# Row sums scaled by ScalarE, small VectorE operations as separate steps, longer DMA pieces and a new order in a fused attention and FFN kernel

## The chip, the cores and the metric

The kernel runs on one core of a Trainium2 chip. The time is device microseconds (us) of one execution, the median of several runs. Five engines work side by side and are ordered by semaphores: TensorE (PE, with its weight loads PEld), VectorE (DVE), ScalarE (ACT), GpSimd (POOL) and SyncE (SP), which issues all DMA transfers here.

## The reference, cut to what matters

```python
# q, k, v: 4 batches x 8 heads x 576 positions x 64
q, k = rotate(q), rotate(k)                       # rotary embedding
attn = softmax(q @ k.T / 8)                       # per batch and head
x = concat_heads(attn @ v)                        # 4 x 576 x 512
xn = (x - mean) / sqrt(var + 1e-6) * g_ln
x = x + relu(xn @ w_ch1) @ w_ch2                  # w_ch1 512 x 2048, w_ch2 2048 x 512
gate = sigmoid(causal_conv5(x, conv_w))           # 5 taps per channel
out = (gate * (x @ w_val)) @ w_out                # 512 x 512 each
```

The weights arrive as 64-bit floats, q, k and v as 32-bit floats.

## The kernel before, in words

**Tiles.** Attention goes batch by batch. A batch has 4 pairs of heads, and its 576 queries are cut in four (128, 128, 128, 192, or with the 192 first in odd batches); a pair and a cut is a part, and a part has two or three tiles of 128 queries by all 576 keys, 144 tiles in all. For a tile PE computes scores into PSUM (`a_scores`; plain 32-bit in batch 0, high and low halves in the others), DVE takes the negated row maximum (`a_max`, L537), ACT the exponential (`a_exp`, L543) and a 16-bit high half (`a_hi`, L549), DVE the low half (`a_lo`, L554), SP issues a DMA transpose (`a_turn`, L559), and PE multiplies the transposed pieces with v and a column of ones (`a_pv`, L578 and L581). The tiles of a part form a group with one PSUM buffer `ov`, of which there is one (ring `so=1`). When a group is complete, `a_rd` drains it on DVE: the row sums, in the column of ones, are scaled with the scale of v (L605), inverted (L606), and the outputs multiplied with them (L610); for the lead tile of 64 queries ACT does the last step (`a_lead`, L624). A second form, `a_sum` on ACT in place of L605, is in the code and not in use (`RD_SUM = 9`, over the highest batch number).

**Weights.** W1 and W2 come as 16 blocks of 1 MB of 64-bit floats (`Conv`, L700). Each block is put together into 32-bit floats by two ACT and one DVE pass (`p1`, `p0`, `p2`), then scaled by powers of two and split into 16-bit high and low halves (`conv_hi`, `conv_lo`). The scales come from bounds that PE and DVE work out; `conv_scale` is a chain of small DVE operations. W1 has two scales, one for each four blocks (`E1 = 2`).

**FFN.** 18 blocks of 128 rows: layer norm (`ln_a` to `ln_d`), a DMA transpose, then four times a first matmul group (`f1`, L882, 48 matmuls), ReLU split into halves (`relu`, `hlo`), and a second matmul group (`f2`, L910, 12 matmuls).

**Tail.** Nine blocks of 256 rows. The gate is a scaled copy on ACT (`gate_a`), four taps on DVE in one step (`gate_b`, L1108), each of which adds to the result of the one before, and a sigmoid on ACT (`gate_c`, L1112). Then come the value projection (`val`, L1121), its product with the gate (L1126), its halves, and the output projection (`proj`, L1148).

**Order.** `Plan` is a planner in Python that runs when the kernel is built. Each piece of work is a step with an engine, an estimated time, a rank, the steps it comes after and the buffers it takes from rings. The planner goes through time: on each engine it takes, of the steps that are ready within `NEAR` us, the one of lowest rank. SP may run `AHEAD` us ahead of what it reckons the wire has moved. The ranks are a constant of the kind (`R_...`) plus the number of the tile or block; loads have a lead (`..._LEAD`) subtracted. A step is indivisible: all its instructions stand together on the engine's queue. The instructions are then issued in the planned order, and each engine works through its own in that order.

**Lines that the change touches.** `pow2_below_inverse` (L137), `vmax0` and `vmax` (L447, L459), `a_sum` and `a_rd` (L590, L597), `conv_scale` (L743), `ln_a` (L832), `norm_scale`, `w_scale` and `x_scale` (L978, L994, L1078), `gate_b` (L1105), the loads `load` and `Conv.load` (L309, L698), and the steps that plan them.

Of the kernel before, what the change touches and what calls it, by code (L numbers as in the profile page):

```python
# [39 lines left out]
R_XB, R_XS = 278.66, -364.59  # L40
# [15 lines left out]
class Plan:  # L56
# [91 lines left out]
def pow2_below_inverse_root(nc, pool, bound, factor, name):  # L148

    m = pool.tile([128, 1], F32, name=name + "_m", tag=name + "_m", bufs=1)  # L150
    nc.vector.tensor_scalar(out=m, in0=bound, scalar1=factor, scalar2=1e-30, op0=ALU.mult, op1=ALU.max)
    nc.vector.reciprocal(out=m, in_=m)
    r = pool.tile([128, 1], F32, name=name + "_r", tag=name + "_r", bufs=1)
    nc.vector.tensor_scalar(out=r.bitcast(I32), in0=m.bitcast(I32), scalar1=1, scalar2=0x7F800000, op0=ALU.logical_shift_right, op1=ALU.bitwise_and)
    return r
# [3 lines left out]
def kernel(ctx: ExitStack, tc: tile.TileContext, qk, v, g_ln, w_ch1, w_ch2, w_val, conv_w, w_out, rope, eye, out):  # L159
    nc = tc.nc  # L160
    B, NP = qk.shape[0], qk.shape[1]
    S = qk.shape[5]
# [4 lines left out]
    DFF = w_ch1.shape[1] // 2  # L167
# [14 lines left out]
    TURN = 1050 * RATE  # L182
# [117 lines left out]
    def plan_prep(p):  # L300
# [17 lines left out]
        def load_half(k):  # L318
# [4 lines left out]
            nc.sync.dma_start(out=st["r", 1][:, :, c], in_=qk[b, pr][:, 1, :, c])  # L323
# [164 lines left out]
        if p < NP:  # L488
            v_abs.append(plan.step(ACT, act(640) + 0.09, r, vabs, after=[x0, x1], uses=[vt, vh], row="vabs"))
            v_rest.append((r, vt, vh, vhi, vlo, vturn, bf))  # L490
            if p == NP - 1:
                x = plan.step(PE, 0.3, R_TINY, vsum0, after=v_abs + [c_c], takes=[hp])
                x = plan.step(DVE, 1.0, r - 8, vmax0, after=[x], takes=[sv0], uses=[hp])
# [10 lines left out]
        x = plan.step(DVE, 0.9, r - 8, vmax, after=[x], takes=[sv], uses=[hp])  # L504
# [92 lines left out]
    def a_rd(g):  # L597
# [6 lines left out]
        if b < RD_SUM:  # L604
            nc.vector.tensor_scalar(out=rd[:, 0:w], in0=ov[:, 0:w, D], scalar1=1e-9 * P_SCALE, scalar2=prep_v(p)["sv"], op0=ALU.add, op1=ALU.mult)  # L605
        nc.vector.reciprocal(out=rd[:, 0:w], in_=rd[:, 0:w])  # L606
        if m and b < RD_ACT:
# [55 lines left out]
    for g, ts in enumerate(groups):  # L663
# [12 lines left out]
        x = plan.step(DVE, (0.2 if b >= RD_SUM else 0.44) + (0 if by_act else m * 0.14 + (0.08 if m else 0)), R_OUT + ts[-1], lambda g=g: a_rd(g), after=[last], takes=[] if b >= RD_SUM else [rd], uses=[so, vf["sv"]] + ([rd] if b >= RD_SUM else []))  # L676
# [15 lines left out]
    class Conv:  # L692
# [50 lines left out]
    def conv_scale(w, e):  # L743
        m = wpool.tile([128, 1], F32, name=f"wn{w}{e}")
        nc.vector.tensor_reduce(out=m, in_=wmax.pop((w, e)), axis=AX.X, op=ALU.max)
        r = pow2_below_inverse_root(nc, wpool, m, 1.08 if w else gmax, f"w{w}{e}")
        if w == 0:
            nc.vector.tensor_scalar(out=sg[:, e], in0=g_sb, scalar1=r, scalar2=ROOT * W1_SCALE, op0=ALU.mult, op1=ALU.mult)
            nc.vector.tensor_scalar(out=s1[:, e:e + 1], in0=r, scalar1=ROOT * W1_SCALE, scalar2=None, op0=ALU.mult)
            if e == E1 - 1:  # L750
                nc.vector.tensor_reduce(out=smin[:, 0:1], in_=s1, axis=AX.X, op=ALU.min)
                inverse(srt, s1)
                nc.vector.tensor_scalar(out=srt, in0=srt, scalar1=smin[:, 0:1], scalar2=ROOT * W2_SCALE, op0=ALU.mult, op1=ALU.mult)
                inverse(smin[:, 1:2], smin[:, 0:1])
        else:
            nc.vector.tensor_scalar(out=s2, in0=srt, scalar1=r, scalar2=None, op0=ALU.mult)
            inverse(scl, r)
            nc.vector.tensor_scalar(out=scl, in0=scl, scalar1=1.0 / (ROOT * W2_SCALE * XN_SCALE), scalar2=smin[:, 1:2], op0=ALU.mult, op1=ALU.mult)

# [14 lines left out]
    for w in range(2):  # L774
# [7 lines left out]
        for e in range(ne):  # L782
            convs = []
            for g in range(per * e, per * e + per):
                if w == 0:
                    src = w_ch1[(g % 2) * 256:(g % 2 + 1) * 256, (g // 2) * 1024:(g // 2 + 1) * 1024].rearrange("(a p) n -> p a n", p=128)
                else:
                    src = w_ch2[g * 256:(g + 1) * 256, :].rearrange("(a p) n -> p a n", p=128)
# [19 lines left out]
            x = scale = plan.step(DVE, 1.15 + 0.4 * (w or e == E1 - 1), r, lambda w=w, e=e: conv_scale(w, e), after=[x, c_g, scale], uses=[hp])  # L808
# [23 lines left out]
    def ln_a(n):  # L832
# [145 lines left out]
    def norm_scale(out, squares):  # L978
        nc.vector.tensor_scalar(out=out.bitcast(I32), in0=squares.bitcast(I32), scalar1=-0.5, scalar2=float((127 + 63 + 15) << 23), op0=ALU.mult, op1=ALU.add)
# [278 lines left out]
```

## Time and profile before

| what | value |
|---|---|
| runs | 729.34, 730.87, 731.23 us; median 730.87 |
| the profiled execution's own time | 732.34 us |
| its span, first to last instruction | 730.5 us |
| mean granted TensorE clock | 0.985 |
| busy PE / DVE / ACT | 666.6 / 628.7 / 469.5 us |
| DMA | 103.63 MB in 240089 packets |

A line such as L605 is the line of the kernel before. "Busy" is the time in which an engine had an instruction at work; matmuls overlap, and their ends are modelled, so a busy PE is not PE at its peak. The granted clock is a share of TensorE's full speed. The chain that ended last is followed back from the last instruction, at each step to what released it. DMA issues are those of SP's queue (SPq), and their times run from issue to landing.

### The profile page before, as it was taken

What the parts mean: (1) busy time and instruction counts of PE and PEld (TensorE: products, weight loads), DVE (VectorE), ACT (ScalarE), POOL (GpSimd) and SP (SyncE); (2) the same over time, 40 slices, a digit from 0 to 9 for tenths busy, and PEclk for the clock granted to TensorE, in tenths of its full rate; (3) what the DMA queues carried; (4) which work ended last, traced back from release to release, by engine and by line L of the source; (5) the groups of instructions that cost most, each with busy time, mean ns of one, the idle gap of its engine ahead of it and who ended that gap; (6) DMA issues with size and microseconds to landing.
All of it is one profiled execution on the core that took longest, in us unless ns stands there. A gap on an engine that the chain in (4) does not pass through costs nothing.

```text
span 730.5 us, 19479 instructions
## 1 busy us (share of the span) xinstructions
PE 666.6 (91%) x7953; PEld 497.8 (68%) x7953; DVE 628.7 (86%) x1396; ACT 469.5 (64%) x854; POOL 16.6 (2%) x40
## 2 busy tenths in 40 slices
PE   3565579999999999999999999999999999999997
PEld 1354468855867977778777877778766556677673
DVE  5978989999889999999999978987556999997683
ACT  3967887896765667666667866555289535442352
POOL 0000000000001000000000000000000000000000
PEclk9998889999999999999999999999999999999999
DMA  8999999667678978788888668875661441321021
GB/s 285 244 207 232 265 275 288 130 132 163 122 131 139 167 158 143 170 155 156 163 167 192 126 119 125 152 119 99 128 193 31 58 76 44 91 66 31 1 73 57
DMA packets 240089, 103.63 MB, mean 142 GB/s; under 512 B 211200, under 2 KB 228608, under 8 KB 240000
## 3 DMA queue, kind: packets, MB, share of 16 engines
q1 hardware_dynamic: 240000, 102.39, 68.2%
q8 instruction: 62, 1.02, 0.5%
q14 instruction: 27, 0.22, 0.1%
HBM read 45.73 MB, written 4.72 MB: 69 GB/s over the span
## 4 chain that ended last, share of the span: by engine, by line
PE 56%; DVE 25%; DMA 10%; ACT 5%; issue 3%; SPq 0%; DVEq 0%; ACTq 0%
PE acc L910 18%; PE hp L882 18%; DMA pT<-p 9%; PE sc L532 6%; DVE gt L1108 5%; PE ov L578 5%; PE po L1148 4%; DVE nmx L537 3%; DVE p L554 3%; PE ov L581 2%; PE pv L1121 2%; DVE wall L770 2%; DVE wall L713 1%; DVE gt L1126 1%; DVE raw L335 1%
## 5 line engine op out<-in xcount | busy, mean ns | idle before, releaser
L882 PE MATMUL hp<-xT,wall 128*128 128x128 f16 x3456 | 205.4, 219 | 2.7 <-DVE wall L770 1.3
L882 PEld LDWEIGHTS <-wall 128*128 128x128 f16 x3456 | 195.4, 98 | 10.0 <-issue 4.5
L910 PE MATMUL acc<-wall,hh 128*128 128x512 f16 x544 | 161.9, 379 | 1.5 <-DVE x L914 1.5
L543 ACT ACTIVATE p<-sc,nmx 128x576 f32<-128x576 f32 x144 | 103.8, 738 | 68.5 <-DVE nmx L537 67.8
L554 DVE SCALAR_TENSOR_TENSOR p<-p,p 128x576 f16<-128x576 f32 x144 | 106.3, 752 | 20.7 <-ACT p L549 20.1
L578 PE MATMUL ov<-vh,pT 128*128 128x65 f16 (+1 forms) x1296 | 95.0, 201 | 24.5 <-DMA pT<-p 21.0
L578 PEld LDWEIGHTS <-pT 128*128 128x128 f16 x1296 | 80.6, 101 | 41.8 <-DMA pT<-p 28.4
L537 DVE TENSOR_REDUCE nmx<-sc 128x1 f32<-128x576 f32 x144 | 104.2, 748 | 0.3
L910 PE MATMUL acc<-wall,hl 128*128 128x512 f16 x272 | 103.1, 379 | 0.0
L549 ACT ACTIVATE p<-p 128x576 f16<-128x576 f32 x144 | 95.5, 679 | 7.0 <-DMA pT<-p 5.8
L910 PEld LDWEIGHTS <-hh 128*128 128x128 f16 x544 | 49.4, 98 | 52.1 <-issue 3.2
L1108 DVE SCALAR_TENSOR_TENSOR gt<-xT,cw,gt 128x256 f32<-128x256 f32 (+4 forms) x192 | 71.7, 414 | 3.7 <-ACT gt L1099 1.1
L581 PE MATMUL ov<-vl,pT 128*128 128x64 f16 (+1 forms) x720 | 69.8, 201 | 0.0
L900 DVE SCALAR_TENSOR_TENSOR hl<-hp,hh 128x512 f16<-128x512 f32 x68 | 46.6, 685 | 15.9 <-ACT hh L894 15.5
L894 ACT ACTIVATE hh<-hp 128x512 f16<-128x512 f32 x68 | 40.2, 591 | 31.1 <-PE hp L882 29.4
L581 PEld LDWEIGHTS <-pT 128*128 128x128 f16 x720 | 54.1, 101 | 4.7
L910 PEld LDWEIGHTS <-hl 128*128 128x128 f16 x272 | 26.6, 98 | 32.1
L1148 PE MATMUL po<-woh,gv 128*128 128x512 f16 x144 | 44.3, 379 | 0.0
L1112 ACT ACTIVATE gt<-gt 128x256 f32<-128x256 f32 x36 | 15.0, 416 | 44.2 <-DVE gt L1108 44.1
L1121 PE MATMUL pv<-xh,wvh 128*128 128x256 f16 x144 | 39.2, 273 | 3.8 <-DVE gt L1126 3.8
L335 DVE TENSOR_TENSOR raw<-raw,rope_sb 128x256 f32<-128x256 f32 (+2 forms) x63 | 41.2, 664 | 1.7 <-DMA raw<-in_qk_dram 1.7
L1121 PE MATMUL pv<-xl,wvh 128*128 128x256 f16 x144 | 39.2, 272 | 0.1
(151 smaller groups left out, 939.9 us busy)
## 6 DMA issues: line engine op xcount, KB each, us to landing
raw<-in_qk_dram SPq DMA_DIRECT2D x15, 576.0 KB, 4.6
raw<-in_qk_dram SPq DMA_DIRECT2D x48, 128.0 KB, 2.9
wall<-in_moe_w_ch_dram SPq DMA_DIRECT2D x6, 1024.0 KB, 6.5
xw<-in_moe_w_ch_dram SPq DMA_DIRECT2D x6, 1024.0 KB, 6.9
vt<-in_v_dram SPq DMA_DIRECT2D x16, 320.0 KB, 3.4
out_dram<-x SPq DMA_DIRECT2D x18, 256.0 KB, 2.0
kk<-in_moe_w_ch_dram SPq DMA_DIRECT2D x4, 1024.0 KB, 6.7
raw<-in_qk_dram SPq DMA_DIRECT2D x16, 192.0 KB, 4.1
```

Source lines behind the costliest of these rows:

```text
L335: nc.vector.tensor_tensor(out=a, in0=a, in1=t, op=ALU.mult)
L537: nc.vector.tensor_reduce(out=nmx, in_=sc[:, :, 0:HS], axis=AX.XY, op=ALU.max, negate=True)
L543: nc.scalar.activation(out=p32.rearrange("p (e n) -> p e n", e=2), in_=sc[:, :, 0:HS], func=ACTF.Exp, bias=nmx)
L549: nc.scalar.activation(out=p16[:, 0], in_=p32, func=ACTF.Copy, scale=P_SCALE)
L554: nc.vector.scalar_tensor_tensor(out=p16[:, 1], in0=p32, scalar=P_SCALE, in1=p16[:, 0], op0=ALU.mult, op1=ALU.subtract)
L578: nc.tensor.matmul(o, pT[:, c], vh[:, 2 * c + hs:2 * c + hs + nh], start=(c == 0), stop=(c == 8))
L581: nc.tensor.matmul(o[..., 0:D], pT[:, c], vl[:, 2 * c + hs:2 * c + hs + nh], start=False, stop=False)
L882: nc.tensor.matmul(hp[:, j], w1[:, u, wl * 512 + o:wl * 512 + o + 128], xT[:, xl * KD + c], start=(i == 0), stop=(i == 3 * KD - 1))
L910: nc.tensor.matmul(st["acc"], lw[:, j], w2[:, f + j, lo * 512:lo * 512 + 512], start=(f + j == 0 and i == 0), stop=(f + j == KF - 1 and i ...
L1108: nc.vector.scalar_tensor_tensor(out=gt[:, c0:c1], in0=xT[:, c, HALO + c0 - s:HALO + c1 - s], scalar=col(KT - 1 - s, c), in1=gt[:, c0:c1], ...
L1121: nc.tensor.matmul(pv, lw[:, d, c * 128:(c + 1) * 128], rx[:, d], start=(n == 0), stop=(n == 3 * KD - 1))
L1148: nc.tensor.matmul(po, lw[:, d, sl], rx[:, d, :], start=(n == 0), stop=(n == 3 * KD - 1))
```

## The change

Four things change together.

1. `RD_SUM` is 1 instead of 9: in batches 1 to 3 ACT scales the row sums as they leave PSUM (`a_sum`: one activation with scale and bias), and DVE only inverts them and multiplies. For the bias each preparation of v in those batches has one more 1-element DVE operation.
2. A new kind of step, a chain: the small DVE operations that were one step become one step each, planned with times of their own, so that the planner can lay other work between them. The instructions are those of before. This holds for the divide by the row sums, the scales of v, of W1, W2, w_val and w_out, the layer norm's statistics, the scale of x in the tail and the gate's taps.
3. The 1 MB weight blocks and the queries are laid out in DRAM by the host so that what one transfer brings to a partition is one piece: 8 KB instead of two of 4 KB, and both halves of a cut of queries together, 1 KB (or 1.5 KB) instead of two of half that.
4. The planner's constants change, and `TURN`, the size with which it reckons a transpose.

```diff
-QS, K_LEAD = 3, -29.14
-T_LAG, RATE, NEAR, AHEAD = 2.4, 280.0, 0.11, 1.58
+QS, K_LEAD = 3, -26.92
+T_LAG, RATE, NEAR, AHEAD = 2.4, 280.0, 0.09, 2.47
-QK_LEAD_0, QK_LEAD, V_LEAD_0, V_LEAD, LD_LEAD, W_LEAD = 247.72, 10.36, -2.03, -1.82, 32.3, 8.41
-R_W1, S_W1, R_W2, S_W2 = 2.7, 0.85, 13.38, 1.42
-R_GAIN, R_TINY, R_LN, R_RELU, R_FO, R_OUT = 98.97, -900, -41.32, -673.25, -182.29, -96.09
-R_SC, R_PV, R_F1, R_F2 = 0, -55.05, 189.81, 461.5
-R_MX, R_EXP, R_LO, R_TURN = -9.93, -10.69, -21.44, -113.65
+QK_LEAD_0, QK_LEAD, V_LEAD_0, V_LEAD, LD_LEAD, W_LEAD = 292.79, 6.66, -9.84, -7.03, 31.11, 12.78
+R_W1, S_W1, R_W2, S_W2 = 2.48, 0.84, 11.82, 0.14
+R_GAIN, R_TINY, R_LN, R_RELU, R_FO, R_OUT = 99.04, -900, -185.75, -491.59, -65.84, -124.82
+R_SC, R_PV, R_F1, R_F2 = 0, -38.66, 347.6, 880.51
+R_MX, R_EXP, R_LO, R_TURN = -19.13, -18.8, -50.27, -88.84
-RD_SUM = 9
-R_TW, R_X3, R_GATE, R_VAL, R_VALD, R_PROJ = 312.89, -180.78, 113.3, 1264.59, -1036.9, -343.96
-R_XB, R_XS = 278.66, -364.59
+RD_SUM = 1
+R_TW, R_X3, R_GATE, R_VAL, R_VALD, R_PROJ = 440.03, -450.32, 188.85, 949.2, -1028.76, -327.56
+R_XB, R_XS = 222.6, -608.98
...
+    def chain(self, eng, times, rank, ops, after=(), takes=(), uses=(), row=None):
+        run = []
+        def part(k):
+            if k == 0:
+                run.append(ops())
+            next(run[0], None)
+        x = None
+        for k, time in enumerate(times):
+            x = self.step(eng, time, rank, lambda k=k: part(k), after=[x] if k else after, takes=() if k else takes, uses=list(uses) + (list(takes) if k else []), row=None if k else row)
+        return x
...
-    TURN = 1050 * RATE
+    TURN = 1150 * RATE
...
-            st["r", n] = t[:, :, 0:S if n else nq]
-            nc.sync.dma_start(out=st["r", n], in_=qk[b, pr][:, n, :, slice(0, S) if n else slice(q0, q1)])
+            o = t.rearrange("p a n -> p (a n)")[:, 0:2 * (S if n else nq)]
+            st["r", n] = o.rearrange("p (a n) -> p a n", a=2)
+            nc.sync.dma_start(out=o, in_=qk[b, pr][:, n, 0:2 * S] if n else qk[b, pr][:, n, 2 * q0:2 * q1])
...
         if b < RD_SUM:
             nc.vector.tensor_scalar(out=rd[:, 0:w], in0=ov[:, 0:w, D], scalar1=1e-9 * P_SCALE, scalar2=prep_v(p)["sv"], op0=ALU.add, op1=ALU.mult)
+            yield
         nc.vector.reciprocal(out=rd[:, 0:w], in_=rd[:, 0:w])
+        yield
...
-            nc.sync.dma_start(out=raw.rearrange("p (a n) -> p a n", a=self.src.shape[1]), in_=self.src)
+            nc.sync.dma_start(out=raw, in_=self.src)
...
-                if w == 0:
-                    src = w_ch1[(g % 2) * 256:(g % 2 + 1) * 256, (g // 2) * 1024:(g // 2 + 1) * 1024].rearrange("(a p) n -> p a n", p=128)
-                else:
-                    src = w_ch2[g * 256:(g + 1) * 256, :].rearrange("(a p) n -> p a n", p=128)
+                src = (w_ch2 if w else w_ch1)[g]
...
         for s, c0, c1 in taps(m):
             nc.vector.scalar_tensor_tensor(out=gt[:, c0:c1], in0=xT[:, c, HALO + c0 - s:HALO + c1 - s], scalar=col(KT - 1 - s, c), in1=gt[:, c0:c1], op0=ALU.mult, op1=ALU.add)
+            yield
...
-            x = plan.step(DVE, sum(dve(c1 - c0) + 0.065 for _, c0, c1 in taps(m)), r, lambda m=m, c=c: gate_b(m, c), after=[x], uses=[xT, gt])
+            x = plan.chain(DVE, [dve(c1 - c0) + 0.065 for _, c0, c1 in taps(m)], r, lambda m=m, c=c: gate_b(m, c), after=[x], uses=[xT, gt])
```

The other chains are made in the same way: a `yield` after each small operation, and `plan.chain` with a list of times in place of `plan.step` with their sum. `pow2_below_inverse_root` goes, and its three operations stand in `conv_scale`.

## Rows read from the trace of the kernel before

**Rows 1.** Page, part 1: engine busy us (share of the span), instructions

```profile
PE 666.6 (91%) x7953; PEld 497.8 (68%) x7953; DVE 628.7 (86%) x1396; ACT 469.5 (64%) x854; POOL 16.6 (2%) x40
```

**Rows 2.** Stretches: start:end, length; busy us (instructions) of PE, PEld, DVE, ACT, POOL; clock; DMA

```profile
60.00:80.00 20.00, 13.93 (x194) 11.58 (x196) 17.94 (x35) 16.53 (x25) 0.00 (x0) 0.83 1.15 257
80.00:100.00 20.00, 10.54 (x137) 8.21 (x138) 16.76 (x43) 14.92 (x22) 0.94 (x1) 0.66 1.11 269
0.00:120.00 120.00, 73.76 (x850) 57.29 (x852) 100.40 (x198) 88.61 (x128) 2.97 (x12) 0.91 1.06 254
180.00:540.00 360.00, 355.54 (x4971) 280.01 (x4970) 315.51 (x698) 234.38 (x433) 11.87 (x22) 1.00 0.79 148
540.00:720.00 180.00, 173.60 (x1458) 116.39 (x1456) 152.36 (x385) 93.25 (x203) 0.00 (x0) 1.00 0.25 54
```

**Rows 3.** Chain that ended last, 0 to 120 us: shares, then start us, us, what

```profile
by line: DMA pT<-p 27.1%; DVE nmx L537 7.5%; DVE p L554 7.4%; DVE wall L770 6.5%; DVE wall L713 5.7%; DMA raw<-in_qk_dram 5.3%; issue 5.1%; PE sc L527 5.0%; ACT p L543 3.5%; DVE raw L333 2.4%; DVE raw L335 2.2%; ACT p L549 2.2%; PE ov L578 
...
32.04 8.27 DMA pT<-p
40.82 9.21 DMA pT<-p
56.46 7.59 DMA pT<-p
85.54 7.47 DMA pT<-p
```

**Rows 4.** The same view, 560 to 730 us: shares by line

```profile
by line: DVE gt L1108 22.4%; PE po L1148 15.1%; PE acc L910 12.2%; PE hp L882 11.0%; PE pv L1121 8.7%; DVE gt L1126 4.3%; issue 4.0%; DVE gv L1136 3.9%; DVE xT L1064 3.8%; DVE xl L1093 3.6%; DVE rope_sb L1052 3.1%; ACT xj L1072 1.8%; DVE x 
```

**Rows 5.** Groups by shape: count, busy us, mean ns, idle us before and its releasers

```profile
L605 DVE TENSOR_SCALAR rd<-ov,sv 128x2 f32<-128x2 f32 x48 | 10.2, 213 | 12.9 <-PE ov L578 12.8
...
L543 ACT ACTIVATE p<-sc,nmx 128x576 f32<-128x576 f32 x144 | 103.8, 738 | 68.5 <-DVE nmx L537 67.8
...
L624 ACT ACTIVATE x<-ov,rd 64x64 f32<-64x64 f32 x32 | 9.8, 307 | 5.1 <-DVE x L610 4.4 <-PE sc L532 0.4
...
L253 ACT ACTIVATE gab<-g_sb 128x4 f32<-128x4 f32 x1 | 0.2, 188 | 0.0
```

**Rows 6.** DVE in order of time, around 27 us: start us, us, instruction

```profile
26.62 0.75 DVE L554 SCALAR_TENSOR_TENSOR p<-p,p 128x576 f16<-128x576 f32 x1
27.29 0.21 DVE L605 TENSOR_SCALAR rd<-ov,sv 128x2 f32<-128x2 f32 x1
27.53 0.17 DVE L606 RECIPROCAL rd<-rd 128x2 f32<-128x2 f32 x1
27.73 0.29 DVE L610 TENSOR_TENSOR x<-ov,rd 128x128 f32<-128x128 f32 x1
27.94 0.75 DVE L537 TENSOR_REDUCE nmx<-sc 128x1 f32<-128x576 f32 x1
```

**Rows 7.** The same view, 699.7 to 703.9 us

```profile
699.74 2.04 DVE L1108 SCALAR_TENSOR_TENSOR gt<-xT,cw,gt 128x256 f32<-128x256 f32 x4
...
702.03 0.75 DVE L1126 SCALAR_TENSOR_TENSOR gt<-pv,gt 128x256 f32<-128x256 f32 x2
```

**Rows 8.** DMA issues: count, KB each, median us from issue to landing

```profile
raw<-in_qk_dram SPq DMA_DIRECT2D x48, 128.0 KB, 2.9
...
out_dram<-x SPq DMA_DIRECT2D x18, 256.0 KB, 2.0
...
kk<-in_moe_w_ch_dram SPq DMA_DIRECT2D x4, 1024.0 KB, 6.7
...
pT<-p SPq DMA_TRANSPOSE x144, 3.6
...
r<-in_moe_w_val_dram SPq DMA_DIRECT2D x4, 512.0 KB, 5.7
```

**Rows 9.** Waits over the whole span: us in total, times, longest us

```profile
DVE rd L605 <- PE ov L578: 13.0, 11, 4.8
...
PE ov L578 <- DVE x L610: 2.5, 1, 2.5
```

More of the change, by code (lines that the diff above doesn't have):

```diff
@@ L161 @@
     B, NP = qk.shape[0], qk.shape[1]
-    S = qk.shape[5]
+    S = qk.shape[4] // 2
     D = 64
@@ L166 @@
     w_ch1, w_ch2, w_val, conv_w, w_out = (a.bitcast(I32) for a in (w_ch1, w_ch2, w_val, conv_w, w_out))
[L167 removed]
+    DFF = w_ch1.shape[0] * 512 // 2
     KD = DM // 128
@@ L492, in plan_prep @@
                 x = plan.step(PE, 0.3, R_TINY, vsum0, after=v_abs + [c_c], takes=[hp])
-                x = plan.step(DVE, 1.0, r - 8, vmax0, after=[x], takes=[sv0], uses=[hp])
+                x = plan.chain(DVE, [0.58, 0.07, 0.08, 0.07], r - 8, lambda: vmax0(), after=[x], takes=[sv0], uses=[hp])
                 for r, vt, vh, vhi, vlo, vturn, f in v_rest:
@@ L503, in plan_prep @@
         x = plan.step(PE, 0.1, R_TINY, vsum, after=[x, c_c], takes=[hp], uses=[vb])
-        x = plan.step(DVE, 0.9, r - 8, vmax, after=[x], takes=[sv], uses=[hp])
+        x = plan.chain(DVE, [0.19, 0.07, 0.08, 0.07] + ([0.07] if b >= RD_SUM else []), r - 8, lambda: vmax(), after=[x], takes=[sv], uses=[hp])
         x = plan.step(ACT, act(640) + 0.1, r - 8, vhi, after=[x], uses=[vt, vh, sv])
@@ L675 @@
             last = plan.step(ACT, 0.26, R_OUT + ts[-1], lambda g=g: a_sum(g), after=[last], takes=[rd], uses=[so, vf["sv"]])
-        x = plan.step(DVE, (0.2 if b >= RD_SUM else 0.44) + (0 if by_act else m * 0.14 + (0.08 if m else 0)), R_OUT + ts[-1], lambda g=g: a_rd(g), after=[last], takes=[] if b >= RD_SUM else [rd], uses=[so, vf["sv"]] + ([rd] if b >= RD_SUM else []))
+        x = plan.chain(DVE, ([] if b >= RD_SUM else [0.13]) + [0.08] + ([] if by_act or not m else [m * 0.14 + 0.1]), R_OUT + ts[-1], lambda g=g: a_rd(g), after=[last], takes=[] if b >= RD_SUM else [rd], uses=[so, vf["sv"]] + ([rd] if b >= RD_SUM else []))
         o = [x]
@@ L807 @@
             x = plan.step(PE, 0.1, R_TINY, lambda w=w, e=e: conv_turn(w, e), after=[x, c_c], takes=[hp])
-            x = scale = plan.step(DVE, 1.15 + 0.4 * (w or e == E1 - 1), r, lambda w=w, e=e: conv_scale(w, e), after=[x, c_g, scale], uses=[hp])
+            x = scale = plan.chain(DVE, [0.19, 0.07, 0.08, 0.07] + ([0.14, 0.07] if w else [0.14] + ([0.14, 0.14] if e == E1 - 1 else [])), r, lambda w=w, e=e: conv_scale(w, e), after=[x, c_g, scale], uses=[hp])
             for g in range(per * e, per * e + per):
@@ L928 @@
         ln, xn, x16, xT, acc = Buf("ln"), Buf("xn"), Buf("x16"), Buf("xT"), Buf("acc")
-        x = plan.step(DVE, 1.0, R_LN + n, lambda n=n: ln_a(n), after=rows[n] + [e_ffn], takes=[ln], row="ln")
+        x = plan.chain(DVE, [0.6, 0.1, 0.07], R_LN + n, lambda n=n: ln_a(n), after=rows[n] + [e_ffn], takes=[ln], row="ln")
         x = plan.step(POOL, 2.0 if n >= LN_ACT else 1.3, R_LN + n, lambda n=n: ln_p(n), after=[x], uses=[ln])
@@ L994, in w_scale @@
     def w_scale(nm):
-        norm_scale(tail["s" + nm], tail["b" + nm])
+        yield from norm_scale(tail["s" + nm], tail["b" + nm])
         if nm == "wo":
@@ L1037 @@
         x = plan.step(PE, 0.15, R_TINY, lambda nm=nm: w_sum(nm), after=w_abs + [c_c], takes=[hp])
-        x = scaled = plan.step(DVE, 0.3 if nm == "wv" else 0.75, r - KD, lambda nm=nm: w_scale(nm), after=[x, scaled], uses=[hp])
+        x = scaled = plan.chain(DVE, [0.1, 0.07] + ([0.14, 0.07] if nm == "wo" else []), r - KD, lambda nm=nm: w_scale(nm), after=[x, scaled], uses=[hp])
         for c, (tb, k) in enumerate(w_bufs):
@@ L1171 @@
         y = plan.step(PE, 0.08, R_TINY, lambda m=m: x_sum(m), after=y + [c_c], takes=[hp], uses=[bb])
-        y = plan.step(DVE, 0.7, R_XS + m, lambda m=m: x_scale(m), after=[y, scaled], takes=[sx], uses=[hp], row="xs")
+        y = plan.chain(DVE, [0.1, 0.07, 0.07, 0.07], R_XS + m, lambda m=m: x_scale(m), after=[y, scaled], takes=[sx], uses=[hp], row="xs")
         h = plan.step(ACT, act(1024), R_X3 + m, lambda m=m: xd(m), after=[last, y], takes=[x3], uses=[xT, sx])
@@ L1231, in key_blocks, with blocks, by_cuts @@
         return a.reshape(B, H // 2, 2, 5, 128, D).transpose(0, 1, 4, 3, 2, 5)
+    def blocks(a):
+        n = 512 if a.shape[0] == H * D else a.shape[1]
+        a = a.reshape(-1, 2, 128, a.shape[1] // n, n).transpose(3, 0, 2, 1, 4)
+        return a.reshape(-1, 128, 2 * n)
+    def by_cuts(a):
+        cuts = lambda b: (0, 192, 320, 448, S) if b % 2 else (0, 128, 256, 384, S)
+        return _np.stack([_np.concatenate([a[b][..., i:j].reshape(H // 2, 2 * D, -1) for i, j in zip(cuts(b), cuts(b)[1:])], axis=-1) for b in range(B)])
     named = [
-        ("qk", _np.stack([feature_major(inputs["q"]), feature_major(inputs["k"])], axis=3)),
+        ("qk", _np.stack([by_cuts(feature_major(inputs["q"])), feature_major(inputs["k"]).reshape(B, H // 2, 2 * D, 2 * S)], axis=3)),
         ("v", key_blocks(inputs["v"])),
         ("moe_g_ln", inputs["moe_g_ln"].reshape(-1, 128).T),
-        ("moe_w_ch1", inputs["moe_w_ch1"]),
-        ("moe_w_ch2", inputs["moe_w_ch2"]),
+        ("moe_w_ch1", blocks(inputs["moe_w_ch1"])),
+        ("moe_w_ch2", blocks(inputs["moe_w_ch2"])),
         ("moe2_w_val", inputs["moe2_w_val"]),
```

52 lines of the change are left out of this document (36 added, 16 removed).

## The prediction, made before the changed kernel was run

> **What bounds the kernel now.** I read the engines' shares first, then the stretches, then the chain that ended last, then single instructions. TensorE (PE) is busy 666.6 of the span's 730.5 us, VectorE (DVE) 628.7, ScalarE (ACT) 469.5 [rows 1]: PE is the fullest, DVE close behind. The reader is to see that these shares are unevenly spread [rows 2]. In 0 to 120 us PE is busy 73.76, so 46.2 us idle; from 180 to 540 it is busy 355.54 of 360 (4.5 idle), from 540 to 720 it is busy 173.60 of 180 (6.4 idle). These are 57 of its 64 idle us, and 46 of them stand at the start. So the middle is PE's: what DVE or ACT save there can return at most 4.5 us.
>
> The start has another limit. DMA stands at 1.06 in 0 to 120, its engines full; PE's granted clock is 0.83 and then 0.66 in 60 to 100, where it is busy only 13.93 and 10.54 of 20 [rows 2]. The chain of these 120 us spends 27.1% on transposes of the probabilities (DMA pT<-p) and near a third on DVE (row maxima, low halves, weights). Its four longest transposes take 8.27, 9.21, 7.59 and 7.47 us [rows 3]: they stand behind 1 MB weight blocks on the same queue. The tail's chain, 560 to 730, gives 22.4% (38 us) to the convolution taps of the gate on DVE, the largest share, and about half to PE [rows 4].
>
> **The change, part by part.** The sum goes against the profiled execution, 732.34 us, which is 1.5 above the median of the three timed runs, 730.87.
>
> *Row sums on ACT.* Batches 1 to 3 have 16 output groups each, so 48 instructions of L605 at 213 ns leave DVE [rows 5]. The next instruction, the reciprocal, starts 0.24 us after it [rows 6], so 48 x 0.24 = 11.5 us of DVE go. Twelve preparations of v gain one 1-element instruction each, priced by the reciprocal's step of 0.20 in the same rows: 12 x 0.20 = 2.4. DVE nets -9.1. ACT gains 48 small activations. The trace has none of this shape; the nearest are L253 (4 elements, 188 ns) and L624 (64 elements out of PSUM, 307 ns) [rows 5], so 9.0 to 14.7 us. All lies in 130 to 540 us, where ACT is busy 234 of 360 and PE 355.5: ACT has room, PE sets the end. The DVE gain can be worth 0 to 4.5; the added wait is priced as a rival below. I take -1.
>
> *Small DVE operations as separate steps.* The instructions are the same; other work may now be laid between two that depend on each other. In the divide by the row sums, L605, L606 and L610 (0.21, 0.17, 0.29 long) start 0.24 and 0.20 apart, a gap of 0.03 after each; the independent L537 behind them starts 0.21 after L610 began, 0.08 before it ended [rows 6]. So a dependent link costs 0.11 us more than an independent one. In the start there are some 45 links (12 groups of 2, two chains of weight scales with 14 together, 3 of the first v scale, 4 of the layer norm): 45 x 0.11 = 5.0 us of DVE. A third of the chain there runs through DVE [rows 3], so about 2 are worth time; bounds 0 and 5. I take -2. In the tail the taps carry it: four dependent taps take 2.04, a step of 0.52; two independent instructions of the same form and size take 0.75, a step of 0.33 [rows 7]. That is 0.19 a tap, for 80 whole taps (five of the nine blocks of 256 rows have no batch border inside, each with 4 column groups of 4 taps; split ones already alternate): 15 us of DVE if each had an independent partner, about half if every second has one. PE's idle time there, 6.4, is the ceiling. I take -4; bounds 0 and 6.4. When this stall goes, PE's own matmuls are late next. The low end is not above zero on DVE: an instruction laid between delays only its own chain, by 0.33 to 0.75, and the sigmoid behind it waits on an ACT that is half idle there [rows 2].
>
> Here the Trainium skill speaks against the change: "VectorE: DVE Perf Modes", The DRAIN you can't avoid, says that after every operation the pipeline is emptied and that chaining operations without semaphores skips none of it. By that rule a separated chain gains nothing. The rows disagree, since 0.33 and 0.52 are different steps.
>
> *Longer pieces.* A weight block of 1 MB was 256 pieces of 4 KB and becomes 128 of 8 KB; a query block of 128 KB was 256 pieces of 512 B and becomes 128 of 1 KB. Bytes stay. Today they land in 6.7 us (kk) and 2.9; an output of 256 KB in 2 KB pieces lands in 2.0, and a 512 KB block of w_val, single 4 KB pieces, in 5.7 [rows 8]. So short pieces look dear for queries, and weights have little to gain. What counts is the time that transposes spend behind them in the start: 8.27 + 9.21 + 7.59 + 7.47 = 32.5 against four times the usual 3.6 [rows 3, 8], so 18 us of queueing. Bounds: half of it, -9, and +2, if an 8 KB piece holds an engine so that a transpose comes in later. I take a tenth, -2, nearest to w_val's row, which says that size of piece hardly tells for weights. Query loads after 120 us stand under PE's work and count nothing.
>
> The skill's "DMA: Bandwidth & Descriptors", Specifications, puts the least size for full rate at 512 B, so by it this term would be zero and the sum 2 us higher; the 2.9 against 2.0 does not fit it well.
>
> *The new order.* The planner's ranks, leads and look-ahead all change, and with them the place of nearly every instruction. PE's preferences stay as they were: scores and products with v ahead of the first and second FFN matmuls. What moves is the start. Maxima and exponentials outrank the conversion of W1 by about 21 tiles instead of 12 or 13, which delays W1; its loads are ranked ahead of later query loads and the queue may run 2.47 us ahead of the wire instead of 1.58, which hurries it. The trace can't price the two. Nearest bounds: PE's idle 15.5 us in 60 to 100, where FFN work for the first rows lacks the second half of W1, is the most that earlier weights give back; eight tiles of attention put ahead, each with a low half and a maximum of 0.75 on DVE (L554, L537) [rows 6], are 12 us of delay, of which PE, idle two fifths of that stretch [rows 2], would lose some 5 to 10. I take 0, between ends that are about alike.
>
> Sum: -1 - 2 - 4 - 2 + 0 = -9; 732.34 - 9 = 723.3; less the 1.5 to the median, 721.9. Forecast **722 us**.
>
> **The rivals.**
>
> *PE absorbs it.* PE is the bound from 120 us on, the start's transposes wait for bytes and not for pieces, and PE's recorded gaps are small. Then only 1 or so is gained: 730. For it: 355.54 of 360 [rows 2]. Against: some two fifths of the tail's chain is DVE [rows 4].
>
> *The start is rearranged well.* Weights come early enough that PE fills its idle 15.5 us in 60 to 100 [rows 2], and with PE busy the clock stays up. Two thirds of it, 10 us, on top of the -9: 732.3 - 19 - 1.5 = 712. For it: a third of PE's idle time stands in these 40 us. Against: DVE is busy 34.7 of the 40 and must convert the weights and do the attention both.
>
> *The row sum on ACT holds up PE (slower).* There is one output buffer in PSUM; the next group's products wait until it is drained. Today DVE drains it alone. Then ACT must come first, in order, behind an exponential of 738 ns [rows 5], and the exponentials and ReLUs behind it wait with it. DVE stood 13.0 us in 11 waits for these products, up to 4.8 each, and PE 2.5 us once for the drain [rows 9]; the 13.0 pass to ACT. A drain is later by up to 0.31 + 0.74 - 0.24 = 0.8 us, 48 times 39 us. It decides where PE has no FFN block at hand to cover it; if that is so for one in four, 10 us, and with -2 of the gains left: 732.3 + 8 - 1.5 = 739. For it: DVE's waits on PE [rows 9]. Against: PE has had FFN work at hand nearly always since 180 us.
>
> *No gain from separated steps.* If every DVE operation starts only after the one before has emptied the pipeline, the -2 and -4 fall away: 728. Against it stand the two steps of rows 7. It is the page's rule named above.
>
> That the new order interleaves nothing, the change not doing what it says, comes to the same 728.
>
> **How the numbers follow.** Forecast 0.44 (its own range 716 to 727), PE absorbs it 0.12, a well arranged start 0.18, the slower ACT 0.20, no gain from separated steps 0.06. A measurement can tell 0.3%, 2.2 us, from no change: 728.7 to 733.1 is "same". Faster: 0.44 + 0.18 + half of 0.06 = 0.65. Same: 0.12 + 0.03 = 0.15. Slower: 0.20, which also holds the order's bad end. The range, 710 to 736, reaches to the good start's 712 and toward the slower 739, and leaves out about one in ten at each side.
>
> **What would show it.** Right: L605 sixteen times on DVE instead of 64, and 48 small activations on ACT of 0.19 to 0.31; taps of two columns alternating at a step near 0.34, and PE's idle time in the tail under 4; fewer transposes over 7 us before 100, and PE's idle time before 120 some 4 to 5 lower. Wrong: PE's idle in 180 to 540 well over 4.5 with waits on the reciprocal or ACT's row sum (the slower rival); taps still 0.5 apart; or PE's idle before 120 changed by over 10 either way, which would make the order the whole story.

## The result, and the profile after

The changed kernel takes **722.08 us** (median of 4 runs, 720.09 to 723.1) against 730.46 us (median of 4) for the kernel before in the same comparison: a ratio of **0.9883**, 95% interval 0.9855 to 0.9911, so 8.4 us faster. The profiled execution took 723.1 us, its span is 721.3. Forecast were 722 us, and 723.3 for a profiled one. The sum came out; several of its terms did not, as the experiments show.

The page's first part of the kernel after: busy us (share of the span) and instructions of each engine, as in [rows 1].

```profile
PE 673.6 (93%) x7953; PEld 504.7 (70%) x7953; DVE 604.0 (84%) x1360; ACT 486.1 (67%) x902; POOL 18.2 (3%) x40
```

DVE lost 24.7 us of busy time and 36 instructions (48 gone to ACT, 12 added for the bias); ACT has 48 more. PE's matmuls are the same 7953, and yet PE is busy 7.0 us longer: the next view says why. The stretches of the kernel after, columns as in [rows 2]: start:end, length; busy us (instructions) of PE, PEld, DVE, ACT, POOL; granted clock; DMA.

```profile
60.00:80.00 20.00, 15.55 (x164) 11.73 (x164) 16.21 (x30) 15.81 (x23) 0.00 (x0) 0.67 1.10 244
80.00:100.00 20.00, 15.30 (x151) 12.15 (x149) 18.74 (x48) 16.46 (x25) 0.55 (x1) 0.67 1.10 268
0.00:120.00 120.00, 83.14 (x810) 62.81 (x810) 100.73 (x204) 91.72 (x135) 2.12 (x12) 0.79 1.06 258
180.00:540.00 360.00, 358.44 (x4980) 280.91 (x4978) 303.03 (x666) 256.45 (x496) 13.36 (x22) 1.00 0.80 149
540.00:720.00 180.00, 174.92 (x1445) 116.86 (x1442) 142.07 (x380) 88.80 (x192) 0.00 (x0) 1.00 0.23 54
```

In 0 to 120 us PE's idle time fell from 46.2 to 36.9, and nothing was gained: the granted clock fell with it, from 0.91 to 0.79, and fewer matmuls were done (810 instead of 850). PE was less idle because it was slower. Idle time therefore doesn't tell how far a kernel has come; the work done does. I counted each form of matmul up to a time and multiplied by the step of that form at full clock, for the forms of the tail read from lines such as these of the chain after (start us, us, what):

```profile
602.21 2.68 PE hp L906 x48
...
607.51 2.59 PE acc L934 x12
610.10 5.18 PE po L1179 x24
```

So a first FFN matmul counts 0.056, a second 0.216, an output projection 0.216; likewise a value projection 0.109, a product with v 0.030 (0.059 with both heads' columns), a score of batches 1 to 3 0.070 (0.148 for a lead tile); batch 0's scores, all done by 180 us, count 0.12 to 0.26. PE's own work done, in us at full clock:

| up to | before | after | ahead by |
|---|---|---|---|
| 180 us | 102.8 | 103.5 | 0.7 |
| 300 us | 214.7 | 219.3 | 4.6 |
| 540 us | 444.5 | 448.9 | 4.4 |
| 640 us | 537.3 | 545.2 | 7.9 |

At 540 us, for example, all attention is done in both kernels, and the changed one has 33 first and 12 second FFN matmuls more: 33 x 0.056 + 12 x 0.216 = 4.4. A second profile of the changed kernel (e5 below) comes to 1.5, 4.6, 5.3 and 8.7, so a figure is good to about 1 us. The start gave next to nothing, the middle about 4, all of it before 300 us, and the tail about 5, which makes up the 9.2 us between the two spans. One line's view says the same for the end, the output projections (count: min/median/max ns, first and last start us): 717.1 us where the last one started at 726.3 before.

```profile
L1179 PE MATMUL po<-woh,gv x144: 379/379/379, 578.5 to 717.1; 128*128 128x512 f16 x144
```

The chain that ended last, 0 to 120 us of the kernel after, against [rows 3]:

```profile
by line: DMA pT<-p 19.9%; ACT p L553 8.5%; issue 8.2%; PE hp L906 8.0%; PE sc L537 7.8%; DMA raw<-in_qk_dram 5.3%; ACT p L559 4.3%; DVE p L564 3.8%; ACT wall L791 3.6%; DVE nmx L547 2.9%; PE ov L588 2.4%; PE bound L741 2.3%; DVE raw L342 2.
...
31.35 7.99 DMA pT<-p
...
53.49 7.82 DMA pT<-p
...
70.64 8.10 DMA pT<-p
79.73 5.04 PE hp L906 x48
```

Three transposes still take about 8 us, where four took 7.5 to 9.2. The last line is a first FFN group of 48 matmuls in 5.04 us, against 2.68 in the tail: the granted clock from 79.7 to 84.8 us was 0.53, so for most of it PE worked at the lower of its two clock levels, 1.2 GHz. And the same view from 560 to 722 us, against [rows 4]:

```profile
by line: PE po L1179 28.8%; PE pv L1152 26.7%; PE acc L934 19.3%; PE hp L906 14.9%; DVE gt L1138 2.7%; DVE xl L1123 1.5%; ACT L1143 0.8%; DVE rope_sb L1080 0.8%; DVE gt L1157 0.5%; DVE xT L1092 0.4%; ACT x L1183 0.4%; DVE gv L1167 0.4%; DVE
```

The taps had 22.4% of this chain and have 2.7%; PE's four matmul lines had 47% and have 90%. The tail is now PE's.

### The profile page after: what moved, and what is told of

Same layout as the page of the kernel before. It is cut to its first block, busy times and chain, and to the rows that moved or that the text cites. A ratio compares the mean times of both kernels' runs of the same rounds, so it can differ in the third digit from the quotient of the medians.

```text
span 721.3 us, 19536 instructions
## 1 busy us (share of the span) xinstructions
PE 673.6 (93%) x7953; PEld 504.7 (70%) x7953; DVE 604.0 (84%) x1360; ACT 486.1 (67%) x902; POOL 18.2 (3%) x40
## 4 chain that ended last, share of the span: by engine, by line
PE 70%; ACT 11%; DVE 10%; DMA 5%; issue 4%; SPq 1%; ACTq 0%; DVEq 0%
PE hp L906 21%; PE acc L934 20%; PE sc L542 7%; PE po L1179 6%; PE pv L1152 6%; PE ov L588 5%; DMA pT<-p 3%; PE ov L591 2%; ACT p L553 2%; DVE p L564 2%; DMA raw<-in_qk_dram 1%; ACT p L559 1%; DVE nmx L547 1%; PE sc L537 1%; ACT wall L791 1%
## 5 line engine op out<-in xcount | busy, mean ns | idle before, releaser
L906 PE MATMUL hp<-xT,wall 128*128 128x128 f16 x3456 | 209.6, 222 | 0.0
L906 PEld LDWEIGHTS <-wall 128*128 128x128 f16 x3456 | 200.2, 99 | 6.2 <-issue 2.7
L1138 DVE SCALAR_TENSOR_TENSOR gt<-xT,cw,gt 128x256 f32<-128x256 f32 (+16 forms) x192 | 68.8, 413 | 1.2 <-ACT gt L1129 1.2
L1152 PE MATMUL pv<-xh,wvl 128*128 128x256 f16 x144 | 39.2, 273 | 0.0
```

The lines of the kernel that those rows point to most:

```text
L906: nc.tensor.matmul(hp[:, j], w1[:, u, wl * 512 + o:wl * 512 + o + 128], xT[:, xl * KD + c], start=(i == 0), stop=(i == 3 * KD - 1))
L1138: nc.vector.scalar_tensor_tensor(out=gt[:, c0:c1], in0=xT[:, c, HALO + c0 - s:HALO + c1 - s], scalar=col(KT - 1 - s, c), in1=gt[:, c0:c1], ...
L1152: nc.tensor.matmul(pv, lw[:, d, c * 128:(c + 1) * 128], rx[:, d], start=(n == 0), stop=(n == 3 * KD - 1))
```

## The experiments

The disputed question: which of the four parts carries the 8 us? The forecast gave the separate steps 6 of 9, the row sums 1, the pieces 2, the order 0. The rivals: the order is the whole story, or the row sums on ACT cost time that something else pays back. The runs were made on three chips, e1 to e4, e5 to e8 and e9 to e12; on each the kernel before ran too (medians 733.07, 732.79 and 731.54 us). Ratios, with a 95% interval, are to that, and a difference of two ratios is given in us of 731. Two ways of taking a part back were used: at a fixed place, where the planned order stays and only what is issued changes, and planned again, where the planner works out an order of its own.

**e1, the row sums back on DVE, order fixed.**

```diff
-        nc.scalar.activation(out=rd[:, 0:w], in_=ovs[g][:, 0:w, D], func=ACTF.Identity, scale=prep_v(p)["sv"], bias=prep_v(p)["se"])
+        nc.vector.tensor_scalar(out=rd[:, 0:w], in0=ovs[g][:, 0:w, D], scalar1=1e-9 * P_SCALE, scalar2=prep_v(p)["sv"], op0=ALU.add, op1=ALU.mult)
```

> The changed kernel with every queue in its order, but the 48 row sums of batches 1 to 3 scaled by a DVE instruction of 0.21 us at the place where ACT's activation of 0.35 us stood. Theory of the prediction (DVE's relief is worth 1 us of the -9): 722 to 724, PE idle in 180 to 540 up by at most 1 to 2 from 1.6. Rival A (the 5 us that the trace after gains in PE's work between 180 and 300 come from this relief): 725 to 728. Rival B (ACT holds the drain up, so that the move cost time): 718 to 721.

Measured 721.0 us, 0.9841 [0.9816, 0.9867]. With the DVE instructions back the kernel is no slower than the changed one (0.9883, and 0.987 in e5): moving the row sums gains nothing by itself.

**e2, every chain issued together at its first step's place, order fixed.**

```diff
             if k == 0:
-                run.append(ops())
-            next(run[0], None)
+                for _ in ops():
+                    pass
```

> The changed kernel with the order of all its queues, but the operations of each chain stand together at the place of the chain's first, so that nothing lies between them. Theory of the prediction (separated steps are worth 6 us, 4 of them in the tail): 726 to 729, taps 0.5 apart again, PE's idle time in 540 to 720 up by 3 or more. Rival (the order of the rest is what gained; DVE has room): 721 to 724.

Measured 743.84 us, 1.0144 [1.0118, 1.0171]. This one edit loses the whole gain and 11 us more, far beyond what either side expected.

**e3, pieces and loads as before (4 KB and 512 B), order fixed.**

```diff
-            nc.sync.dma_start(out=o, in_=qk[b, pr][:, n, 0:2 * S] if n else qk[b, pr][:, n, 2 * q0:2 * q1])
+            nc.sync.dma_start(out=st["r", n], in_=qk[b, pr][:, n, :, slice(0, S) if n else slice(q0, q1)])
...
-            nc.sync.dma_start(out=raw, in_=self.src)
+            nc.sync.dma_start(out=raw.rearrange("p (a n) -> p a n", a=self.src.shape[1]), in_=self.src)
```

> The changed kernel with weights and queries laid out in DRAM as before: two pieces of 4 KB and of 512 B (or 768 B) a partition in place of one of 8 KB and 1 KB. The order of the queues is the same. Theory of the prediction (longer pieces worth 2 us in the start): 723 to 725, PE's work done by 180 us some 2 us less. Rival (the start's transposes wait for bytes and the start gained nothing in the trace after): 721.5 to 722.5. Rival (a longer piece holds the engines longer): 719 to 721.

Measured 720.31 us, 0.9832 [0.9808, 0.9857]. In this profile four of the sixteen weight blocks (`kk`) landed later, in 7.9 us against 6.2, the other two groups as before (7.9 against 7.7 and 6.2 against 6.4); e12, with the same old pieces, has 6.9 for `kk`. No loss shows in the time: the longer pieces are worth nothing.

**e4, the planner's constants of before, with separate steps, pieces and row sums as changed.**

```diff
-T_LAG, RATE, NEAR, AHEAD = 2.4, 280.0, 0.09, 2.47
+T_LAG, RATE, NEAR, AHEAD = 2.4, 280.0, 0.11, 1.58
...
-    TURN = 1150 * RATE
+    TURN = 1050 * RATE
```

> The changed kernel with row sums on ACT, separate steps and longer pieces, planned with the constants of the kernel before (ranks, leads, look-ahead, reckoned size of a transpose). Theory of the prediction (the order is worth nothing by itself): 721 to 724. Rival (the constants carry most of the gain): 727 to 733; if they were in balance only with the old steps it may be slower than before.

Measured 728.08 us, 0.9946 [0.9924, 0.9967]: 5.6 us of the gain (0.9946 against e5's 0.987, times 731) need the new constants. The other three parts together, with the constants of before, gain 3.9.

**e5, the changed kernel once more**, to have it on a chip with the next three.

> The changed kernel itself, beside the next three on the same chip. Both theories: 719 to 723, ratio to the kernel before 0.983 to 0.989; it sets the mark for the others.

Measured 722.34 us, 0.987 [0.9846, 0.9894]. It is the base for what follows.

**e6, each chain as one step again, planned again.**

```diff
-        run = []
...
-        x = None
-        for k, time in enumerate(times):
-            x = self.step(eng, time, rank, lambda k=k: part(k), ...)
-        return x
+        return self.step(eng, sum(times) + 0.06 * (len(times) - 1), rank, lambda: [None for _ in ops()], ...)
```

> The changed kernel with each chain planned and issued as one step again (time: the sum plus 0.06 us a link), everything planned anew with the new constants. The first round's run with the chains together in a fixed order lost 22 us, part of which may be the place where they stood. Theory (separate steps are worth about 6 us, DVE's dependent links): 726 to 730. Rival A (they carry all and more; the new constants need them): 733 to 745. Rival B (with a plan of its own one step does as well): 720 to 723.

Measured 733.95 us, 1.0028 [1.0009, 1.0048]. Row sums, pieces and constants together, without the separate steps, leave the kernel 2 us slower than before; with these constants the separate steps are worth 11.6 us (1.0028 against 0.987) even where the planner works out an order without them. The constants were not chosen anew for the one-step form, so 11.6 is not what the steps are worth against the best plan without them.

**e7, the row sums on DVE, planned again.**

```diff
-RD_SUM = 1
+RD_SUM = 9
```

> The changed kernel with the row sums of all batches on DVE (RD_SUM 9), planned anew. Theory after the first round (DVE has room where these stand; the fixed-order run lost nothing): 719 to 724. Rival (a plan that knows of the row sum gains from it): 725 to 729.

Measured 724.7 us, 0.9897 [0.987, 0.9924]: 2 us more than e5, between the two expectations, with intervals that overlap.

**e8, the kernel before with the new constants alone** (the constants of the diff shown ahead of the prediction, `RD_SUM` still 9).

> The kernel before (row sums on DVE, chains as one step, old pieces) with the new constants alone. Theory (order worth 0 by itself): 728 to 733. Rival A (the order carries the gain, as the run with old constants at 728 suggests for 6 to 7 of 10 us): 722 to 726. Rival B (the new constants need the separate steps): over 733.

Measured 739.7 us, 1.011 [1.0085, 1.0134]. By themselves the new constants cost 8 us: they need the separate steps.

**e9, only the taps together, at the first tap's place; e10, all other chains together; e11, the taps together at the last tap's place.** All three keep the order.

```diff
-    def chain(self, eng, times, rank, ops, after=(), takes=(), uses=(), row=None):
+    def chain(self, eng, times, rank, ops, after=(), takes=(), uses=(), row=None, at=None):
...
+            if at is not None:
+                if k == at % len(times):
+                    for _ in ops():
+                        pass
+                return
```

(e9 passes at=0 for the taps, e11 at=-1; in e10 the default is 0 and the taps pass None.)

> The changed kernel with the order of all its queues, only the four (or eight) taps of a gate together at the place of the first; all other chains stay apart. In the run with all chains together PE fell 10 us of its own work behind in 540 to 660 and 8 before 540. Theory (separated taps carry the tail's share): 730 to 734, nothing lost before 540. Rival (the tail's gain is the order's, DVE has room there): 722 to 725.

> The changed kernel with the order of all its queues, the taps apart, but the operations of all other chains (row sums, scales, layer norm) together at the place of the first. Theory (these links hold DVE up by 0.11 us each, some 5 us in the whole start and as much in the middle): 727 to 732, lost before 540. Rival (they are short and cost little; the taps carried the 22): 722 to 725.

> As the run with the taps together at the first's place, but together at the place of the last. If what costs is that a chain holds DVE while others wait, both places cost alike, 728 to 736. If it is the place (operations pulled ahead of their turn), this one costs less than 3: 722 to 725. If a later gate is what hurts, it costs more than the first place.

Measured: e9 734.84 us, 1.0036 [1.0014, 1.0058]; e10 732.99 us, 1.0012 [0.9988, 1.0036]; e11 736.79 us, 1.0073 [1.0046, 1.0099]. Against e5's 0.987 the taps are worth 12 us at the first place and 15 at the last, the other chains 10; together 22, where both at once cost 20 (e2, 1.0144 less 0.987, in the same terms). The intervals of e9 and e11 overlap, so the place matters little, and neither kind of chain carries the gain alone.

Their profiles also show where the time goes. The stretches of e9 (columns as above), one of them short, then its waits of PE from 540 us on (total us, times, longest):

```profile
180.00:540.00 360.00, 359.18 (x4986) 281.31 (x4984) 302.79 (x665) 256.91 (x498) 13.01 (x22) 1.00 0.79 148
540.00:740.00 200.00, 177.94 (x1424) 117.58 (x1422) 148.36 (x379) 85.57 (x190) 0.00 (x0) 0.98 0.21 48
574.00:578.00 4.00, 4.00 (x14) 1.60 (x12) 3.27 (x8) 0.73 (x4) 0.00 (x0) 0.57 0.00 0
```

```profile
PE pv L1157 <- DVE gt L1162: 3.5, 3, 1.9
PE acc L939 <- DVE x L943: 3.2, 1, 3.2
PE hp L911 <- DVE sx L1008: 2.7, 2, 2.4
...
```

And the waits of PE in the kernel after, from 540 us on:

```profile
PE hp L1011 <- ACT xj L1100: 0.9, 3, 0.6
PE acc L934 <- DVE x L938: 0.7, 1, 0.7
PE hp L1011 <- DVE oq L744: 0.6, 1, 0.6
PE hp L1011 <- ACT woh L1014: 0.3, 1, 0.3
```

To 540 us e9 is the changed kernel (449.8 of PE's work done, as in e5). From there to the end of its span of 733.1 us PE is idle 193.1 - 177.9 = 15.2 us, against 181.3 - 174.9 = 6.4: 8.8 more. The other 3.0 of the 11.8 us between the two spans are PE's own: the same work keeps it busy 177.9 instead of 174.9 us, at a granted clock of 0.98. The short stretch shows where: right after the wait of 3.2 us the clock was 0.57.

The three waits make 9.4, and none is a wait for a tap: they are for DVE instructions of other work, an FFN addition (`x`), a scale (`sx`) and a product with the gate, that are late behind taps in one piece. How long such a piece is shows DVE in e9 in order of time (start us, us, instruction; pieces of one line run together as xN, under the first one's form), with what stands behind it, and at the same form in the kernel after:

```profile
570.67 2.03 DVE L1143 SCALAR_TENSOR_TENSOR gt<-xT,cw,gt 128x255 f32<-128x255 f32 x4
572.62 0.74 DVE L943 SCALAR_TENSOR_TENSOR x<-acc,scl,x 128x512 f32<-128x512 f32 x1
...
590.20 4.26 DVE L1143 SCALAR_TENSOR_TENSOR gt<-xT,cw,gt 128x64 f32<-128x64 f32 x16
594.37 0.73 DVE L1097 COPY xT<-tx 128x1024 uint16<-128x1024 uint16 x1
594.99 0.41 DVE L1162 SCALAR_TENSOR_TENSOR gt<-pv,gt 128x256 f32<-128x256 f32 x1
...
608.55 2.04 DVE L1143 SCALAR_TENSOR_TENSOR gt<-xT,cw,gt 128x256 f32<-128x256 f32 x4
...
622.70 4.13 DVE L1143 SCALAR_TENSOR_TENSOR gt<-xT,cw,gt 128x256 f32<-128x256 f32 x12
626.74 0.42 DVE L1172 TENSOR_TENSOR gv<-gt,gv 128x256 f16<-128x256 f32 x1
627.07 0.15 DVE L1008 TENSOR_SCALAR sx<-hp 128x1 int32<-128x1 int32 x1
```

```profile
691.21 0.49 DVE L1138 SCALAR_TENSOR_TENSOR gt<-xT,cw,gt 128x256 f32<-128x256 f32 x1
691.60 0.43 DVE L1157 SCALAR_TENSOR_TENSOR gt<-pv,gt 128x256 f32<-128x256 f32 x1
691.93 0.43 DVE L1167 TENSOR_TENSOR gv<-gt,gv 128x256 f16<-128x256 f32 x1
692.27 0.49 DVE L1138 SCALAR_TENSOR_TENSOR gt<-xT,cw,gt 128x256 f32<-128x256 f32 x1
...
695.07 4.83 DVE L1138 SCALAR_TENSOR_TENSOR gt<-xT,cw,gt 128x256 f32<-128x256 f32 x12
```

In e9 DVE is held for about 2 us by the taps of one gate, and for over 4 where two gates stand in a row; PE's waits of 3.2, 1.9 and 2.4 us end with the `x`, the product and the `sx` behind the pieces shown. After, a product or a half slips in behind one tap of 0.49. The twelve at 695 us stand (4.83 - 0.48) / 11 = 0.40 apart, so none follows the tap that it depends on; four dependent ones stand 0.52 apart in both e9 and [rows 7]. So two things were saved, 0.11 us of DVE a link and the waits of others behind a piece. e9 puts both back at once. In the piece at 590 us, whose sixteen taps are split at a batch border and alternate, no link costs anything (they stand 0.26 apart at lengths of 0.27 and 0.41), and the piece at 570 has three links, 0.33 us: in these two waits the holding is most of it. How much is whose over the whole tail is open.

In the profile of e10 the loss lies in the middle. Its stretches:

```profile
180.00:540.00 360.00, 355.13 (x4929) 277.71 (x4927) 307.63 (x662) 251.28 (x485) 12.06 (x22) 1.00 0.78 149
540.00:740.00 200.00, 180.38 (x1509) 120.90 (x1505) 146.80 (x385) 94.12 (x204) 0.00 (x0) 0.99 0.21 50
```

PE is idle 4.9 us from 180 to 540, near the 4.5 of before [rows 2] and not the 1.6 of after, and DVE is busy 4.6 us longer. PE's work done is 0.7 behind the changed kernel at 180 us and 5.5 behind at 540 (443.4 against 448.9); after that the two run alike. The profiled execution, 728.86 us, is the fastest of e10's twelve, 4 us under their median: where the rest of the 10 us went, no profile shows.

**e12, e1 and e3 together**, since both lay a little under the changed kernel.

> The changed kernel with two of its parts undone in a fixed order, which each came out at or below it: the old pieces in DRAM, and the row sums on DVE at the place of ACT's activation (the bias operations are left out as well, 12 fewer). If the two add up: 716 to 720, faster than both kernels. If both were scatter: 720 to 723. If DVE lacks the room: 724 or more.

Measured 723.13 us, 0.9889 [0.9859, 0.9919]. The two small differences were scatter between comparisons: no version tried beats the changed kernel clearly, and kernels that differ by nothing that counts lay from 720.3 to 723.1, with ratios from 0.983 to 0.989, a wider spread than one interval.

## Why the prediction was right, and where only its sum was

**The separate steps** were named the largest term, -6; that is right in kind, and no single size fits. With the constants of before they, the row sums and the pieces together gave 3.9 us (e4); with the new constants the steps carry 11.6 against one step planned again (e6) and 20 against the fixed order (e2). The prediction priced a link, 0.11 us, by the DVE time it saves. That number held: the taps' own time stayed (481 ns), their step fell from 0.52 to 0.40. The 0.33 taken for an independent pair was a wrong yardstick; that instruction (L1126) reads the PSUM tile `pv`, the taps only SBUF, and lasts 0.42. So a tap saves 0.12 and not 0.19. What the pricing left out is what an indivisible step does to the others on its engine: the three waits of e9, and the lower clock after the longest.

**Its places** were wrong in part. The start was to give -2 from the steps and -2 from the pieces; by the work done at 180 us it gave 0.7, no more than two profiles of the changed kernel differ by, and the 5.0 us that its links were to save on DVE don't show (busy 158.89 us before, 158.94 after, to 180 us). PE's idle time before 120 us was to fall by 4 to 5; it fell by 9.4, at the lower clock. The middle was given -1, for the row sums alone. It gave about 4, within the 4.5 of PE's recorded idle time, and e10 shows that the small chains gave it, not the row sums (e1). Links of the row sums' divide in batches 1 to 3 and of the v scales stand there too, and the prediction counted only those of the start. The tail was to give -4 and gave about 5, and the taps left its chain as foreseen. PE's idle time there, 5.1 of 180, stayed above the "under 4" that I asked for.

**Row sums on ACT**, -1: the runs show from +2 (e1, 0.9841 against 0.987) to -2 (e7), nothing that they can tell from 0. (The x48 of [rows 5] is the narrow form in all batches; batches 1 to 3 have 36 of it and 12 wide ones. Both last 213 ns, so the sum stands.) Part of the working held: DVE's busy time from 180 to 540 us fell by 12.5, forecast 9.1, and the small chains put together in e10 bring 4.6 of it back; of its 13.0 us of waits for the products [rows 9], ACT now has 10.1. These are the groups of the kernel after (count, busy, mean ns, idle before) and the two waits:

```profile
L605 ACT ACTIVATE rd<-ov,se,sv 128x2 f32<-128x2 f32 x36 | 12.6, 349 | 9.6 <-PE ov L588 9.3
...
L605 ACT ACTIVATE rd<-ov,se,sv 128x4 f32<-128x4 f32 x12 | 4.2, 353 | 1.0 <-PE ov L588 0.8
...
L615 DVE TENSOR_SCALAR rd<-ov,sv 128x2 f32<-128x2 f32 x12 | 2.6, 215 | 0.8 <-PE ov L588 0.7
```

```profile
ACT rd L605 <- PE ov L588: 10.1, 18, 2.0
...
PE ov L588 <- DVE x L622: 3.6, 3, 2.0
```

One activation took 0.35 us, above my upper bound of 0.307; all 48 make 16.8 us of ACT instead of 9.0 to 14.7. The bound was taken from rows with other operands (L624 [rows 5] has a scale per partition, this one a scale and a bias). The Trainium skill would have priced it: "ScalarE: Activation LUTs", What ACT_TABLE_LOAD costs, gives 186 ns plus 0.833 ns a column, and about 93 ns more for each operand read by pointer; with two that is an estimate of 374 ns, and the trace's 349 is nearer to it than to my bound. It changed nothing that shows: ACT is busy 256 of the middle's 360 us. **The slower rival** (ACT's drain holds up PE, 739 us) needed more PE idle time in the middle; it fell from 4.5 to 1.6 us, and PE's waits for the drain, 3.6 us in all against 2.5 [rows 9], all lie before 180 us.

**Longer pieces**, -2: 0 (e3). Query blocks land in 2.7 us against 2.9 [rows 8], the four `kk` blocks of W2 in 6.2 against 6.7, but the six `wall` blocks in 7.7 against 6.5; transposes in 3.7 against 3.6. DMA issues of the kernel after (count, KB, median us to landing):

```profile
raw<-in_qk_dram SPq DMA_DIRECT2D x48, 128.0 KB, 2.7
...
kk<-in_moe_w_ch_dram SPq DMA_DIRECT2D x4, 1024.0 KB, 6.2
...
pT<-p SPq DMA_TRANSPOSE x144, 3.7
```

The price was put on queueing behind 1 MB blocks, and the blocks are as large as before: DMA's share in the first 120 us is 1.06 in both. Here the Trainium skill's 512 B ("DMA: Bandwidth & Descriptors", Specifications), by which the term is zero, agrees with e3, and my reading of 2.9 against 2.0 does not.

**The order**, 0: wrong. Alone on the old steps the new constants cost 8 us (e8); with the separate steps they are worth 5.6 (e4). An order is not a term of a sum: it is good for the steps that it was made for.

That the sum came out at 722 is luck in part: a middle that was under-counted by 3 and a tail by 1 made up for a start and pieces that were to give 4 and gave next to nothing.

**The rival of no gain from separated steps** (728 us) rested on the rule that a DVE operation empties the pipeline whether or not it is chained. The steps of 0.40 and 0.52 decide against the rule, and the 12 to 15 us of e9 and e11 against the rival. The page of the Trainium skill that I cited, "VectorE: DVE Perf Modes", says itself, in the same section, that an operation which is not held starts earlier; I had weighed only the first half. **PE absorbs it** (730 us) fell in the middle, where PE still had about 4 us to give, and in the tail, where it had 5; **a well arranged start** (712 us) did not come.

Not settled: whether the lower clock in the start ate a gain there. The granted clock of 0 to 180 us was 0.86 in the first profile of the changed kernel and 0.91 in e5, at medians of 722.08 and 722.34, and PE's work done at 180 us was 0.8 higher in e5: that bounds the effect at about 1 us between these two profiles, but no run held the clock and changed only the start. And the kernels that were planned again (e4, e6, e7, e8) each have an order of their own, so their differences hold some us of chance that an interval over executions doesn't show.

## What to carry to other kernels

An indivisible step of small dependent operations costs more than its own length: before pricing it by the time that its engine saves, list who stands behind it on that engine and which engine waits for them (here the three waits of e9, 9.4 us). Measure progress by the bound engine's work done, form by form, and not by its idle time, which shrinks when its clock falls. And where an order is worked out by a planner, take parts back both at a fixed place and planned again: the first shows what the order relies on, the second what the part is worth.

## What the runs showed of the hardware

- Four dependent VectorE taps (128x256, 32-bit, all in SBUF) start 0.52 us apart, taps of several columns in turn 0.40, each 0.48 long either way.
- A ScalarE activation of 2 or 4 elements a partition out of PSUM, with scale and bias per partition, takes 0.35 us, nearly twice the 0.188 of L253 [rows 5].
- PE can be idle less and do no more: 9.4 us less idle before 120 us at a granted clock of 0.79 instead of 0.91, and about the same work done (48.6 us of it against 49.3). In the changed kernel's 60 to 100 us PE was busy 15.6 and 15.3 of 20 and was granted 0.67, that is, part of the time at 1.2 GHz.
- In e9 PE waited 3.2 us near 570 us; in the 4 us from 574 it was busy throughout at a granted clock of 0.57, and had 1.00 again from 578. The twelve second FFN matmuls behind the wait took 4.44 us on the chain, against 2.59 at full clock.
- The longest transposes on the chain of the start, issued behind 1 MB loads on the same queue, took 7.8 to 8.1 us against a median of 3.7, with pieces of 8 KB; with pieces of 4 KB 7.5 to 9.2 (before, [rows 3]).
